# First product of each feed-forward layer by Strassen's scheme, with its operands kept in DRAM scratch

## Chip, cores and metric

The kernel runs on one core of one Trainium2 chip. The metric is the device time of one execution in microseconds (us). Three runs of the kernel before took 867.92, 869.43 and 870.33 us; the median is 869.43 us.

## What is computed

A causal retention over 4 sequences of 576 tokens, 8 heads of 64, and behind it two feed-forward layers (512 to 2048 to 512 features) on all 2304 tokens:

```python
scores = scale * np.matmul(q, k.transpose(0, 1, 3, 2))
ret = scores * Dmat[None, :, :, :]          # gamma ** (i - j) for i >= j, else 0
x = (ret @ v) as 2304 x 512
h = x @ w_in;  g = h * sigmoid(h);                              x = g @ w_out      # layer 0
h = x @ w_in;  g = np.maximum(h, 0) + alpha * np.minimum(h, 0); x = g @ w_out      # layer 1
```

The weights arrive as 64-bit floats and everything is computed to float32.

## The kernel before

**Matmuls.** Every float32 operand of the layers is split into a high part in the type fp32r and the rest, low, in the same type (ACT makes the high part by a copy, DVE the low one by a subtraction). A product is then three matmuls, high·high, low·high and high·low, each 128x128 stationary against up to 512 moving columns, accumulated in PSUM.

**Tiles and groups.** The 2304 tokens are five tiles (`TILES`, one of 256 and four of 512). Hidden features come as 16 blocks of 128 (`f`), in groups (`GROUPS`): 2, 4, 4, 4, 2 blocks in layer 0 and four times 4 in layer 1. Each group walks over all tiles, there and back. For a tile and a block, `h_unit` (L491) makes one PSUM bank of h from 4 feature chunks (12 matmuls), activates it (ACT and DVE) and splits the result g. `y_unit` (L519, layer 0, tokens as columns) and `out_unit` (L536, layer 1, 512 features as columns) multiply g by the second weights and add the group's sum to `bufb` or `bufa` on DVE (ACT copies it in the first group). The units of g are issued behind the h units of the next tile, so PE has a tile's work in hand while ACT and DVE activate.

**Weights.** `weight` (L328) loads a block of 512 KB as raw words (queue SP), makes floats of it with two ACT, three DVE and one POOL instruction (`low` by `top`), and splits it with one ACT and two DVE instructions. 64 blocks are decoded in all. `split_x` and `split_block` split the activations.

**Attention.** 18 blocks of 128 tokens run ahead of and between the units of the first group. Each loads two packs of 512 KB, is prepared on DVE, multiplied in 64x64 matmuls and split by `split_block` (L482).

**Order.** Everything is recorded by `Program` (L52) in the order of the code. PE keeps that order. For ACT, DVE, POOL and SP a planner (`order`, L144) sets each engine's order from costs and due times: of the instructions that can begin first it takes the one that is due first. It treats DVE instructions that read SBUF alone and POOL's as not running at once (`held`). `close_att` (L304) issues what is recorded so far and gives the attention's memory to the layers. Since the planner's wrapper issues all instructions, all have line 228 in the profile, and tiles tell them apart.

## Time and profile before

| | |
|---|---|
| runs | 867.92, 869.43, 870.33 us |
| profiled execution, first to last instruction (span) | 866.1 us |
| PE busy | 841.1 us (97%) |
| DVE busy | 618.9 us (71%) |
| ACT busy | 428.6 us (49%) |
| POOL busy | 94.4 us (11%) |
| DMA | 58.34 MB, mean 67 GB/s |

The profiled execution's own device time is not listed beside its span; the median of the runs is 3.3 us over the span. Busy shares are averages over the whole span; the first 110 us are attention mixed with the first group, the rest is the layers alone.

### The profile page before, as it was taken

The numbers are of one execution on the slowest core, as the hardware profiler recorded it, in microseconds if no ns is written. First come the engines' busy times: TensorE is split into PE (matmuls) and PEld (weight loads), VectorE is DVE, ScalarE is ACT, GpSimd is POOL, SyncE is SP. The second block draws the span as 40 slices with busy tenths as digits, with TensorE's granted clock in tenths as the row PEclk, the third lists the DMA queues.
The fourth block names the chain that finished last, engine by engine and source line by source line (L and its number), as shares of the span: only waits on it lengthen the run. The fifth ranks groups of instructions, "written<-read, shape, count | busy, mean of one in ns | idle before, by whom it ended". The sixth has DMA issues, their size and how long they took to land.

```text
span 866.1 us, 14498 instructions
## 1 busy us (share of the span) xinstructions
PE 841.1 (97%) x5932; PEld 707.6 (82%) x5932; DVE 618.9 (71%) x1015; ACT 428.6 (49%) x819; POOL 94.4 (11%) x68
## 2 busy tenths in 40 slices
PE   5799999999999999999999999999999999999998
PEld 4677788888988888888988888888888788888887
DVE  6988989748894798646899844884459964964443
ACT  3545575424653455324645755774344754543331
POOL 0101112101120022101001100220002210100000
PEclk9899999999999999999999999999999999999999
DMA  9856312201210032100111110220002210001111
GB/s 346 289 188 194 124 59 88 74 0 38 85 49 25 25 98 78 44 1 28 51 44 50 31 43 1 97 74 25 1 1 74 73 49 1 25 1 49 50 50 73
DMA packets 17490, 58.34 MB, mean 67 GB/s; under 512 B 2064, under 2 KB 2320, under 8 KB 17424
## 3 DMA queue, kind: packets, MB, share of 16 engines
q1 hardware_dynamic: 17424, 57.43, 19.3%
q8 instruction: 46, 0.75, 0.3%
q14 instruction: 20, 0.16, 0.1%
HBM read 52.70 MB, written 4.72 MB: 66 GB/s over the span
## 4 chain that ended last, share of the span: by engine, by line
PE 92%; DVE 4%; DMA 3%; ACT 1%; issue 1%; SPq 0%; DVEq 0%
PE bank L228 88%; DMA pack<-in_qkv 3%; PE xo L228 2%; PE sd L228 1%; DVE a L228 1%; DVE att L228 1%; DVE pack L228 1%; DVE w L228 0%; ACT bufa L228 0%; DVE g L228 0%; ACT x L228 0%; DVE act L228 0%; DVE top L228 0%; ACT act L228 0%; DVE x L228 0%
## 5 line engine op out<-in xcount | busy, mean ns | idle before, releaser
L228 PE MATMUL bank<-x,w 128*128 128x512 f32 (+1 forms) x1320 | 280.6, 369 | 1.1 <-ACT x L228 1.1
L228 PEld LDWEIGHTS bank<-x,w 128*128 128x128 f32 x1320 | 230.7, 189 | 43.1 <-ACT x L228 1.3
L228 POOL TENSOR_TENSOR low<-low,top 128x512 f32<-128x512 f32 x64 | 94.2, 1477 | 665.8 <-DVE top L228 625.6
L228 ACT ACTIVATE act<-bank 128x512 f32<-128x512 f32 (+1 forms) x160 | 88.3, 552 | 96.4 <-PE bank L228 92.8
L228 PE MATMUL bank<-x,w0b 128*128 128x512 f32 (+1 forms) x600 | 127.3, 368 | 0.0
L228 PEld LDWEIGHTS bank<-x,w0b 128*128 128x128 f32 x600 | 105.1, 189 | 19.0
L228 DVE SCALAR_TENSOR_TENSOR act<-down,nalpha_sb,act 128x512 f32<-128x512 f32 (+1 forms) x80 | 57.8, 723 | 74.1 <-ACT act L228 73.2
L228 ACT ACTIVATE down<-bank 128x512 f32<-128x512 f32 (+1 forms) x80 | 44.4, 555 | 127.7 <-PE bank L228 126.6
L228 DVE TENSOR_TENSOR bufb<-bank,bufb 128x512 f32<-128x512 f32 (+1 forms) x80 | 50.7, 635 | 43.5 <-PE bank L228 43.0
L228 PE MATMUL bank<-g,w 128*128 128x512 f32 (+1 forms) x336 | 77.9, 371 | 3.0 <-DVE g L228 1.4
L228 DVE TENSOR_TENSOR bufa<-bank,bufa 128x512 f32<-128x512 f32 (+1 forms) x55 | 37.4, 679 | 58.5 <-PE bank L228 58.3
L228 DVE TENSOR_TENSOR act<-bank,act 128x512 f32<-128x512 f32 (+1 forms) x80 | 50.7, 633 | 28.7 <-ACT act L228 28.2
L228 PEld LDWEIGHTS bank<-g,w 128*128 128x128 f32 x336 | 58.3, 195 | 14.4 <-DVE g L228 3.2
L228 ACT ACTIVATE top<-raw 128x512 f32<-128x512 f32 x64 | 42.6, 671 | 39.9 <-POOL low L228 30.6
L228 DVE TENSOR_TENSOR g<-act,g 128x512 fp32r<-128x512 f32 (+1 forms) x84 | 57.1, 684 | 6.7 <-ACT g L228 6.3
L228 PE MATMUL bank<-gb,w1b 128*128 128x512 f32 (+1 forms) x288 | 61.4, 354 | 0.0
L228 ACT ACTIVATE low<-raw 128x512 f32<-128x512 uint32 x64 | 42.7, 672 | 37.4 <-DVE w L228 22.5
L228 ACT CAST g<-act 128x512 fp32r<-128x512 f32 (+1 forms) x84 | 48.6, 581 | 18.4 <-DVE act L228 18.1
L228 PE MATMUL bank<-w,g 128*128 128x512 f32 x240 | 55.7, 390 | 0.4 <-DVE w L228 0.4
L228 PE MATMUL bank<-w1b,gb 128*128 128x512 f32 (+1 forms) x252 | 55.6, 379 | 0.0
L228 PEld LDWEIGHTS bank<-gb,w1b 128*128 128x128 f32 x288 | 48.6, 189 | 7.6
L228 DVE TENSOR_TENSOR x<-bufa,x 128x512 fp32r<-128x512 f32 (+1 forms) x82 | 53.1, 676 | 1.3 <-ACT x L228 1.3
(55 smaller groups left out, 1065.7 us busy)
## 6 DMA issues: line engine op xcount, KB each, us to landing
raw<-in_w SPq DMA_DIRECT2D x64, 512.0 KB, 3.5
pack<-in_qkv SPq DMA_DIRECT2D x26, 512.0 KB, 4.9
bufb<-in_qkv SPq DMA_DIRECT2D x10, 512.0 KB, 5.7
out<-bufa SPq DMA_DIRECT2D x17, 256.0 KB, 2.0
att<-in_small SPq DMA_DIRECT2D x1, 256.0 KB, 2.5
out<-bufa SPq DMA_DIRECT2D x2, 128.0 KB, 1.7
alpha_sb<-in_alpha SPq DMA_DIRECT2D x1, 8.0 KB, 5.6
```

Source lines behind the costliest of these rows:

```text
L228: getattr(getattr(self.nc, name), method)(*args, **kwargs)
```

## The change

The first product of each layer, but for the first two hidden blocks of layer 0, is made in units of 256 hidden features (`q`, a pair of blocks) and 768 tokens (`p`, three of them, two halves of 384). Weights and activations are cut into 2 x 2 blocks; seven block products (`product`, 6 matmuls of 384 columns each) give what eight gave. Four of the seven weight operands and four of the seven activation operands are sums or differences, formed on DVE ahead of the split. The sums of products are made partly by accumulating in PSUM, partly by three ACT copies and two DVE additions in each unit (`unit`).

- The seven activation operands (`xops`, one set) are made when a layer first meets a token group and stored in DRAM (`od`); later groups load them back. Layer 0's activations themselves go through DRAM (`xd`), one store in each attention block, one load for each token group.
- The first two hidden blocks of layer 0 run as before, on six tiles of 384 tokens. `y_unit` and `out_unit` become pieces that a queue hands out: `gaps` says how many pieces `fill` issues behind each product. Pieces of layer 0 have 384 columns, those of layer 1 still 512.
- POOL adds the low word to each decoded weight (one more POOL instruction a block); DVE then needs one subtraction for the split where it needed two instructions.
- Two short matmuls stand ahead of the first unit and touch its two PSUM banks.

```diff
-GROUPS = [(0, range(0, 2)), (0, range(2, 6)), (0, range(6, 10)), (0, range(10, 14)), (0, range(14, 16)),
-          (1, range(0, 4)), (1, range(4, 8)), (1, range(8, 12)), (1, range(12, 16))]
-TILES = [256, 512, 512, 512, 512]
-RAWS = 2
+GROUPS = [(0, [0]), (0, [1, 2]), (0, [3, 4]), (0, [5, 6]), (0, [7]),
+          (1, [0, 1]), (1, [2, 3]), (1, [4, 5]), (1, [6, 7])]
+HALF = 384
+NT6 = NT // HALF
+NPR = NT6 // 2
+BPP = 2 * HALF // P
...
+A22, A11, A12, S3, S1, S2, S4 = range(7)
+B11, T1, B21, T2, B22, T3, T4 = range(7)
...
+        nc.gpsimd.tensor_tensor(out=dst, in0=dst, in1=low, op=ALU.add)
...
+    def weights(layer, q, plain=False):
...
+        w = rings["wt"].next()
+        decode(layer, 0, 2 * q, w[:, 512:1024])
+        decode(layer, 0, 2 * q + 1, w[:, 0:512])
...
+        both = rings["w0"].next().rearrange("p (s n) -> p s n", s=2)
+        a21, a22, a11, a12 = (w[:, i * 256:(i + 1) * 256] for i in range(4))
+        split(both[:, 0, 0:768], both[:, 1, 0:768], w[:, 256:1024])
+        nc.vector.tensor_tensor(out=a22, in0=a21, in1=a22, op=ALU.add)
+        nc.vector.tensor_tensor(out=a21, in0=a11, in1=a21, op=ALU.subtract)
+        nc.vector.tensor_tensor(out=a11, in0=a22, in1=a11, op=ALU.subtract)
+        nc.vector.tensor_tensor(out=a12, in0=a12, in1=a11, op=ALU.subtract)
+        split(both[:, 0, 768:1792], both[:, 1, 768:1792], w)
+        w_pair[layer, q] = both
...
+        nc.sync.dma_start(out=home[:, :, n % BPP * P:(n % BPP + 1) * P], in_=block(n))
...
+    def operands(src):
+        b11, b12, b21, b22 = (src[:, 2 * k:2 * k + 2, j * HALF:(j + 1) * HALF] for k in range(2) for j in range(2))
+        def put(i, b):
+            hi, lo = (xops[i][:, s * 2 * HALF:(s + 1) * 2 * HALF].rearrange("p (k t) -> p k t", k=2) for s in range(2))
+            split(hi, lo, b)
+        def less(out, a, b):
+            nc.vector.tensor_tensor(out=out, in0=a, in1=b, op=ALU.subtract)
+        put(B11, b11)
+        less(b11, b12, b11)
+        put(T1, b11)
+        put(B21, b21)
+        put(B22, b22)
+        less(b12, b22, b12)
+        less(b22, b22, b11)
+        put(T2, b22)
+        put(T3, b12)
+        less(b21, b21, b22)
+        put(T4, b21)
...
+    def operands_for(layer, p, first):
+        if first:
+            if layer == 0:
+                nc.sync.dma_start(out=xs, in_=xd[p])
+                operands(xs.rearrange("p (c t) -> p c t", c=NC))
+            else:
+                operands(feat(p))
+            for i in (B11, T1, B21, T2, B22, T3, T4):
+                nc.sync.dma_start(out=od[layer][p][i], in_=f32(xops[i]))
+        elif loaded[-1] != (layer, p):
+            for i in (B11, T1, B21, T2, B22, T3, T4):
+                nc.sync.dma_start(out=f32(xops[i]), in_=od[layer][p][i])
...
+    def product(o, both, a, b, start=False):
+        w = both[:, :, a * 2 * P:(a + 1) * 2 * P]
+        x = xops[b].rearrange("p (s k t) -> p s k t", s=2, k=2)
+        for k in range(2):
+            wh, wl = (w[:, s, k * P:(k + 1) * P] for s in range(2))
+            xh, xl = x[:, 0, k], x[:, 1, k]
+            nc.tensor.matmul(o, wh, xh, start=start and k == 0, stop=False, skip_group_check=True)
+            nc.tensor.matmul(o, wl, xh, start=False, stop=False, skip_group_check=True)
+            nc.tensor.matmul(o, wh, xl, start=False, stop=k == 1, skip_group_check=True)
+    def unit(layer, q, key, fill, gaps):
+        weights(layer, q)
+        both = w_pair[layer, q]
+        f1, f2 = 2 * q, 2 * q + 1
+        a, b, d = home("a"), home("b"), home("d")
+        product(a, both, A11, B11, start=True)
+        nc.scalar.copy(b, a)
+        fill(gaps[0])
+        product(d, both, S1, T1, start=True)
+        s5 = rings["act"].next()
+        nc.scalar.copy(s5, d)
+        fill(gaps[1])
+        product(a, both, A12, B21)
+        activate(layer, f1, (*key, 0), a)
+        fill(gaps[2])
+        product(b, both, S2, T2)
+        s2 = rings["act"].next()
+        nc.scalar.copy(s2, b)
+        fill(gaps[3])
+        product(d, both, S4, B22)
+        nc.vector.tensor_tensor(out=d, in0=d, in1=s2, op=ALU.add)
+        activate(layer, f1, (*key, 1), d)
+        fill(gaps[4])
+        product(b, both, S3, T3)
+        nc.vector.tensor_tensor(out=s5, in0=b, in1=s5, op=ALU.add)
+        activate(layer, f2, (*key, 1), s5)
+        fill(gaps[5])
+        product(b, both, A22, T4)
+        activate(layer, f2, (*key, 0), b)
...
+                weight(0, f)
+            weights(0, 1)
...
+    for n, (gi, layer, qs, p) in enumerate(steps):
+        first = GROUPS[gi - 1][0] != layer or gi == 1
+        operands_for(layer, p, first)
...
+        now = with_done(woven(early[:3], 3) + flat(early[3:]), early_key, fs)
+        then = with_done(flat(late), late_key, fs)
+        if len(qs) == 2:
+            unit(layer, qs[0], (gi, p), fill, (0, 1, 1, 0, 1, 2) if layer == 0 else (0, 1, 1, 0, 1, 1))
+            queue += now[:3]
+            unit(layer, qs[1], (gi, p), fill, (1, 1, 1, 0, 1, 2) if layer == 0 else (1, 1, 0, 0, 1, 2))
+            queue += now[3:]
+            fill(len(queue))
+            queue += then```

How the change moves instructions, at three places. Names: `bank`, `sd` and `xo` are PSUM, `xop_1878` to `xop_1884` are the operands B11, T1, B21, T2, B22, T3, T4, `g` the activated h, `w` second weights (and, with `xop`, first ones), `shared` the memory of the first group's x and first weights, which later holds two of the three sets of first weights.

**PE, where the first group ends.** Before, the pieces of the last tile are followed by the h matmuls of group 1:

```order
L228 MATMUL bank_110<-g_99,w_2_87 128x512
L228 MATMUL bank_110<-g_99,w_3_88 128x512
L228 MATMUL bank_110<-g_100,w_2_87 128x512
L228 MATMUL bank_107<-x_93,w0b_1734 128x512
L228 MATMUL bank_107<-x_93,w0b_1735 128x512
L228 MATMUL bank_107<-x_94,w0b_1734 128x512
```

Now:

```order
L221 MATMUL bank_152<-g_140,w_2_127 128x384
L221 MATMUL bank_151<-shared 128x384 x12
L221 MATMUL bank_152<-shared 128x384 x12
L221 MATMUL sd<-shared 128x384 x2
L221 MATMUL bank_149<-xop_1878,w_0_124 128x384 x6
L221 MATMUL xo<-xop_1879,w_0_124 128x384 x6
L221 MATMUL bank_150<-g_141,w_0_125 128x384
```

The h matmuls of the last plain tile (24 on `shared`) stand directly ahead of the first block product. Their g is used only behind the second product.

In the second unit of the same step, with the queue of pieces empty, the last products stand without a piece between them:

```order
L221 MATMUL sd<-xop_1881,shared 128x384 x6
L221 MATMUL xo<-xop_1882,shared 128x384 x6
L221 MATMUL sd<-xop_1883,shared 128x384 x6
L221 MATMUL sd<-xop_1884,shared 128x384 x6
L221 MATMUL bank_151<-gb_1891,w_8_133 128x384
L221 MATMUL bank_151<-gb_1891,w_9_134 128x384
```

Three of the four write the same bank of `sd`, which ACT and DVE read in between.

**SP, the same stretch.** Before, behind the last packs only weights are loaded:

```order
L228 DMA bufb<-in_qkv 128x1024 x2
L228 DMA pack_116<-in_qkv 128x1024 x2
L228 DMA raw_68<-in_w 128x512
L228 DMA alpha_sb<-in_alpha 128x16
L228 DMA raw_69<-in_w 128x512
```

Now:

```order
L221 DMA pack_160<-in_qkv 128x1024 x2
L221 DMA xd_72<-xs 512x1x128 x5
L221 DMA raw_115<-in_w 128x512
L221 DMA raw_116<-in_w 128x512
L221 DMA alpha_sb<-in_alpha 128x16
L221 DMA xs<-xd_70 128x3072
L221 DMA raw_115<-in_w 128x512
L221 DMA raw_116<-in_w 128x512
L221 DMA od_0_0_73<-xop_1878 128x1536
```

The load of the first token group stands behind the stores of the last attention blocks and two weight blocks; the stores of the operands follow it on the same queue.

**DVE, the first operands.** Before, h's second tile needs four splits (`x_96<-bufa`) for 48 matmuls:

```order
L228 TENSOR_TENSOR w0b_1737<-a_76,low_72 128x512
L228 TENSOR_TENSOR x_96<-bufa,x_95 128x512
L228 TENSOR_TENSOR act_106<-bank_110,act_106 128x512
L228 TENSOR_TENSOR x_96<-bufa,x_95 128x512 x3
L228 TENSOR_TENSOR g_102<-act_105,g_101 128x512
```

Now:

```order
L221 TENSOR_TENSOR xop_1878<-xs,xop_1878 128x768
L221 TENSOR_TENSOR xs<-xs 128x2x384
L221 TENSOR_TENSOR xop_1882<-xs,xop_1882 128x768
L221 TENSOR_TENSOR xs<-xs 128x2x384
L221 TENSOR_TENSOR xop_1879<-xs,xop_1879 128x768
L221 TENSOR_TENSOR xop_1880<-xs,xop_1880 128x768
L221 TENSOR_TENSOR xs<-xs 128x2x384
```

The second product's operand (T1, `xop_1879`) is the fifth of these instructions, the third's (`xop_1880`) the sixth.

## Rows read from the trace of the kernel before

**Rows 1.** The page: busy time by engine, and the chain's shares by engine.
```profile
PE 841.1 (97%) x5932; PEld 707.6 (82%) x5932; DVE 618.9 (71%) x1015; ACT 428.6 (49%) x819; POOL 94.4 (11%) x68
PE 92%; DVE 4%; DMA 3%; ACT 1%; issue 1%; SPq 0%; DVEq 0%
```
**Rows 2.** Busy time by stretch: PE, PEld, DVE, ACT, POOL, granted clock, DMA.
```profile
27.50:55.00 27.50, 21.73 (x536) 18.22 (x536) 24.44 (x46) 14.71 (x33) 2.86 (x2) 0.88 0.64 222
140.00:650.00 510.00, 510.00 (x2443) 430.65 (x2442) 363.23 (x595) 255.64 (x479) 57.23 (x40) 1.00 0.13 43
650.00:700.00 50.00, 49.58 (x253) 42.16 (x252) 47.37 (x79) 31.09 (x64) 12.36 (x7) 1.00 0.21 73
```
**Rows 3.** The chain in order of time: start, us, what.
```profile
53.53 4.92 DMA pack<-in_qkv
...
110.14 559.81 PE bank L228 x2688
...
679.52 183.53 PE bank L228 x842
```
**Rows 4.** Timeline of PE, 200 to 245 us: start, us, what, count.
```profile
204.24 1.52 PE L228 MATMUL bank<-g,w1b 128*128 128x512 f32 x6
205.60 1.52 PE L228 MATMUL bank<-gb,w 128*128 128x512 f32 x6
...
222.39 0.88 PE L228 MATMUL bank<-g,w 128*128 128x256 f32 x6
223.11 0.88 PE L228 MATMUL bank<-gb,w1b 128*128 128x256 f32 x6
```
**Rows 5.** Groups of instructions, shapes apart: busy us, mean ns; idle before.
```profile
L228 PE MATMUL bank<-x,w 128*128 128x512 f32 x1056 | 246.7, 390 | 1.1 <-ACT x L228 1.1
L228 PEld LDWEIGHTS bank<-x,w 128*128 128x128 f32 x1320 | 230.7, 189 | 43.1 <-ACT x L228 1.3 <-DVE x L228 0.4
...
L228 PE MATMUL bank<-x,w0b 128*128 128x512 f32 x480 | 112.1, 389 | 0.0
```
**Rows 6.** Timelines of POOL and DVE in two places: start, us, what.
```profile
312.56 1.66 POOL L228 TENSOR_TENSOR low<-low,top 128x512 f32<-128x512 f32 x1 [0.42 <-DVE top L228]
...
312.99 1.78 DVE L228 TENSOR_TENSOR a<-a,w1b 128x512 f32<-128x512 f32 x1
...
332.48 0.69 DVE L228 TENSOR_TENSOR gb<-act,gb 128x512 fp32r<-128x512 f32 x1
333.08 0.69 DVE L228 TENSOR_TENSOR act<-bank,act 128x512 f32<-128x512 f32 x1
```
**Rows 7.** Groups of instructions of ACT, DVE and POOL, shapes apart.
```profile
L228 POOL TENSOR_TENSOR low<-low,top 128x512 f32<-128x512 f32 x64 | 94.2, 1477 | 665.8 <-DVE top L228 625.6 <-ACT bufa L228 27.3 <-ACT g L228 8.1
L228 DVE TENSOR_TENSOR act<-bank,act 128x512 f32<-128x512 f32 x64 | 44.0, 687 | 25.9 <-ACT act L228 25.5
L228 DVE TENSOR_TENSOR a<-a,w1b 128x512 f32<-128x512 f32 x16 | 20.4, 1292 | 0.0
L228 ACT CAST x<-bufb 128x512 fp32r<-128x512 f32 x56 | 32.4, 625 | 0.0
L228 DVE TENSOR_TENSOR act<-bank,act 128x256 f32<-128x256 f32 x16 | 6.7, 417 | 2.8 <-ACT act L228 2.8
L228 ACT CAST x<-bufb 128x256 fp32r<-128x256 f32 x12 | 4.5, 405 | 0.0
```
**Rows 8.** DMA: GB/s in 40 slices of 0:110 us; issues, us to landing.
```profile
GB/s 120 275 340 408 386 414 425 402 419 273 225 331 305 313 215 212 45 301 76 203 183 258 174 292 280 149 40 174 180 231 209 305 310 279 28 189 13 0 6 0
raw<-in_w SPq DMA_DIRECT2D x64, 512.0 KB, 3.5
out<-bufa SPq DMA_DIRECT2D x17, 256.0 KB, 2.0
```

More of the change, by code (lines that the diff above doesn't have):

```diff
@@ new lines, in h_unit @@
+    def h_unit(t, f):
+        hi, lo = x_hi[t], x_lo[t]
+        weights(0, f // 2, plain=True)
+        both = w_pair[0, f // 2]
+        o = psum()[:, 0:HALF]
+        for c in range(NC):
+            at = 512 * (1 - f % 2) + c * P
+            wh, wl = both[:, 0, at:at + P], both[:, 1, at:at + P]
+            nc.tensor.matmul(o, wh, hi[:, c], start=c == 0, stop=False)
+            nc.tensor.matmul(o, wl, hi[:, c], start=False, stop=False)
+            nc.tensor.matmul(o, wh, lo[:, c], start=False, stop=c == NC - 1)
+        activate(0, f, (0, t), o)
@@ L585, in retention_ffn_kernel @@
     att_tables()
-    hs, ys = zip(*(unit_pair(s) for s in range(len(TILES))))
     blocks = iter(range(NBLK))
@@ new lines, in retention_ffn_kernel, with fill @@
+    for i in range(2):
+        nc.tensor.matmul(homes["b"][i], first_w0[:, 0, 0:P], x_hi[NT6 - 1][:, 0], start=True, stop=True,
+                         skip_group_check=True)
+    steps = []
+    for gi, (layer, qs) in list(enumerate(GROUPS))[1:]:
+        order = range(NPR) if gi == 1 else [e[3] for e in steps[-NPR:]][::1 if GROUPS[gi - 1][0] != layer else -1]
+        steps += [(gi, layer, qs, p) for p in order]
+    queue = []
+    def fill(n):
+        while n and queue:
+            n -= 1
+            queue.pop(0)()
@@ new lines, in with_done, with woven, flat @@
+    def with_done(pieces, key, fs):
+        return pieces[:-1] + [lambda: (pieces[-1](), done(key, fs))]
+    queue += with_done(y, (0, NT6 - 1), [0, 1])
+    def woven(units, n):
+        out = []
+        for i in range(0, len(units), n):
+            for parts in zip(*units[i:i + n]):
+                out += parts
+        return out
+    def flat(units):
+        return [e for u in units for e in u]
+    for n, (gi, layer, qs, p) in enumerate(steps):
+        first = GROUPS[gi - 1][0] != layer or gi == 1
+        operands_for(layer, p, first)
+        fs = [f for q in qs for f in (2 * q, 2 * q + 1)]
+        halves = []
+        for th in range(2):
+            key = (gi, p, th)
+            if layer == 0:
+                e = [y_pieces(key, fs, p, th, m, len(qs)) for m in range(NC)]
+            else:
+                e = [out_pieces(key, fs, p, th * 3 + b, n == len(steps) - 1 and th == 0 and b == 2) for b in range(3)]
+            halves.append((e, key))
+        (late, late_key), (early, early_key) = halves
+        now = with_done(woven(early[:3], 3) + flat(early[3:]), early_key, fs)
[6 more added lines that the diff above has]
+            fill(len(queue))
+            queue += then
+        else:
+            unit(layer, qs[0], (gi, p), fill, (1, 1, 1, 0, 1, 2))
+            fill(len(queue))
+            queue += now
+            if [e[0] == gi for e in steps[n + 1:n + 3]] != [True, False]:
+                fill(len(queue))
+            queue += then
@@ L620, in retention_ffn_kernel @@
+    fill(len(queue))
     nc.issue()
```

295 lines of the change are left out of this document (149 added, 146 removed).

## The prediction, made before the change was run

> **What bounds the kernel now.** I read the page first: PE is busy 97% of the span, and the chain that ended last is PE for 92% [rows 1]. A busy PE need not be a full one, so the next question is whether it ever waits. In the chain in order of time PE runs for 559.8 us and for 183.5 us without a break; the attention ahead of that still has waits for DMA [rows 3]. From 140 to 650 us PE is busy 510 of 510 us at granted clock 1.00, which is the level of 2.4 GHz; DVE is busy for 363 of these (71%) and DMA for 0.13. The one dense stretch in which PE loses something, 650 to 700 us, is that in which DVE comes to 47.4 of 50 us [rows 2]. So in the layers time is PE's columns and nothing else, and the nearest other limit is DVE.
>
> What a matmul costs is read from the timeline, between starts: 1.36 us for six of 512 columns, 226.7 ns each; 0.72 us for six of 256, 120.0 ns each [rows 4]. Two widths give a line: 106.7 ns for 256 columns (2.4 a ns) and 13.3 ns for each matmul. At 384 columns that is **173.3 ns**. (The mean of 390 ns in the groups [rows 5] is a duration that overlaps its neighbours', not a price.)
>
> **What PE saves.** Before, the loops give 3156 matmuls of 512 columns (1536 of them h's, [rows 5]) and 600 of 256, the last output counted as halves: 3156 x 226.7 + 600 x 120.0 = 787.5 us. Now the order has 3186 of 384 (45 units x 42 = 1890, 144 of the plain first group, 1152 pieces of layer 0), 852 of 512 and 24 of 256: 3186 x 173.3 + 852 x 226.7 + 24 x 120.0 = 748.1 us. The columns fall by 103,680 (43.2 us at 2.4 a ns), and 306 more matmuls take 4 us of it back: **-39.3 us**. The two short matmuls ahead of the first unit count for nothing.
>
> **What lies beside PE.** *DVE.* Durations of 687 ns at 512 columns and 417 at 256 [rows 7] give 0.55 us at 384 and 0.96 at 768; two starts are 0.60 us apart where one lasts 0.69 [rows 6], so a queue of them moves 0.09 faster. Added: 90 additions in units (50 us); operands, 66 instructions of 768 (63 us) where some 130 splits of x by layers went; one DVE instruction for two in 64 decodes. Priced by pitch, all rows of DVE in the order come to 540 us before and 564 now, +24. POOL has 64 instructions more. A POOL instruction holds up a DVE one that meets it: 1.78 us for one that began while POOL was at work [rows 6], 1292 ns on average against 687 for the group that meets it most [rows 7], so up to 0.6 x 64 = 39 us. DVE goes from 619 us to at most 682, some 80% of the new span: not the bound on average, but it must be early where PE waits for it. *ACT* gains three PSUM copies a unit, 135 x 0.5 = 67 us, on 429 busy: covered by its idle half.
>
> *Reloads.* 84 loads of 786 KB. Each operand has one tile, so its load starts when the second unit's product has read it, and must land before the next step's first unit: 102 matmuls lie between (36 products' and 66 pieces'), 17.7 us in layer 0, 17.1 in layer 1. A 512 KB load lands in 3.5 us, and slices of DMA reach 425 GB/s [rows 8]; all seven take 12.9 us at that rate, each in turn. Cover of 17 us against a landing of 3.5 to 8: nothing. Without it, each load would cost its 5 us. The 42 stores run beside PE too, in steps of 31 us.
>
> **What comes back onto the path.** Four places, each with both ends.
>
> 1. *Attention*: 18 stores of 256 KB (`xd`) on SP between the packs. Nothing, if the packs wait for their buffers anyway; 0.62 us of transfer at 425 GB/s and some 0.33 of issue each, 18 x 0.95 = 17 us, if all lie on the path. The chain there is mostly compute, with waits such as 4.9 us for a pack [rows 3]; I take **+4**.
> 2. *The first unit.* From the last block's copy: store 2.0 us [rows 8], load of 1.57 MB (3.7 us of transfer and the 2.3 that a 512 KB load takes beyond its 1.2), two weight blocks ahead on SP (2.5), ACT split 0.83 (from 625 and 405 ns, [rows 7]): 11.3 us. PE has 42 matmuls meanwhile, 7.3 us. So 2 to 4 us, 3 taken. Then T1's low part is DVE's fifth instruction (4.4 us) and wanted 2.2 us after B11's high part: 2. In the second unit no piece stands between the last products: DVE's addition (0.55) and the activation of f2 (2.6 us against 1.7 of cover) cost 2. Sum **+7**; 3 if SP's weights come early, 16 if DVE comes to it with other work and the clock falls with the wait, as in the stretch at 0.88 [rows 2], worth 3 us.
> 3. *Layer 1's first group.* DVE's rows from one operand set to the next come to 29.3 us, 31.7 with two decodes' POOL meetings, for 30.9 us of PE. About 1 us in each of three steps, **+3**; 0 to 12.
> 4. *Every other unit.* Before the last product, DVE must have read that bank: 0.55 us behind whatever it is doing (up to 0.87), with 2.08 us of pieces as cover in layer 0 and 1.36 or 2.72 in layer 1. Only a meeting with POOL breaks it; POOL is at work a fifth of the time. 0.13 us x 45 units = **+6**; 0 to 44 (below).
>
> Sum against the profiled execution: 866.1 - 39.3 + 4 + 7 + 3 + 6 = 846.8 us of span; with the 3.3 us by which the median stands over the span, **850.1 us**.
>
> On place 4 the Trainium skill, "SBUF — State Buffer", section "SBUF: two separate sides", goes further than I do: VectorE with two SBUF inputs and GpSimd share a port pair under an exclusive lock, and the loser waits for the whole instruction. The trace agrees on the single meeting (1.78 us, rows 6). By that rule alone the 64 added instructions at 1.48 us would shut DVE out for 95 us instead of 39, and the rival that goes slower would be the likelier one; the rows' averages are what I go by.
>
> **The rivals.**
> - *All of it hidden.* DVE has 29% idle in the dense stretch, pieces cover each read, and only the first unit waits: 866.1 - 39.3 + 3 + 3.3 = 833 us. For it: not one wait of PE in 510 us [rows 2]. Against it: before, ACT and DVE had a tile's work as cover, now 1 to 2 us. **0.15**
> - *DVE locked at the gates: slower.* In each unit the addition that frees the bank for the last product meets a POOL instruction: 1.78 + 0.55 against 1.36 of cover, 0.98 us in each of 45 units, 44 us: 866.1 - 39.3 + 4 + 7 + 3 + 44 + 3.3 = 888 us. It decides against the change from (39.3 - 14) / 45 = 0.56 us a unit. For it: POOL's doubled work, and 47 of 50 us of DVE where PE does wait [rows 2]. Against it: the planner keeps such instructions apart as far as its costs are right, and waits need a coincidence. **0.13**
> - *DMA in the way.* Stores delay the packs by the full 17 us and the first unit by 16: 866.1 - 39.3 + 17 + 16 + 3 + 6 + 3.3 = 872 us, no change to measure; half as bad, 859. For it: slices of 400 GB/s in the first 25 us [rows 8]. Against: from 27 us on DMA is busy for two thirds at most. **0.11**
> - *The narrow matmul is no cheaper.* A weight load takes 189 ns [rows 5]; if it set the pace under 384 columns, 3186 x 15.7 ns = 50 us come back, 900 us. Against it: at 256 columns the pace is 120 ns with the same loads [rows 4]. **0.03**
>
> **How the numbers follow.** The forecast, 850.1 us, has 0.58, with 840 to 860 from the small terms. What a measurement of this kernel can tell from no change is 0.3%, 2.6 us. Faster: 0.58 + 0.15 + half of DMA's case = 0.79. Same: the worse half, 0.05. Slower: 0.13 + 0.03 = 0.16. The range leaves out slower (0.16) and a few hundredths at the low end, and reaches from just under the first rival to the worse half of DMA: 831 to 872 us.
>
> **What would show it.** Starts of six 384-column matmuls 1.04 us apart; the sum of PE's matmuls at 748 us. One hole of 3 to 8 us in PE behind the attention, released by `xop0` from DMA `xs`; short ones behind `sd` released by DVE. No PE wait released by DMA `xop`. DVE at about 80%. I am wrong if PE's idle time in the layers exceeds some 40 us, if 384 columns take more than 180 ns, or if the attention ends later than 115 us plus a few.

## The result, and the profile after

The changed kernel takes 879.43 us (median of 4 runs, 877.18 to 881.21); the kernel before took 869.21 us beside it. The ratio is 1.0106, 95% interval 1.0078 to 1.0134: slower by 1%, outside the predicted range. The profiled execution took 877.18 us, the fastest of the four, with a span of 875.5 us, 9.4 us more than before. The forecast is set against the traces by one measure, used in all that follows. For each 128x128 matmul of n columns, the time from its start to the next matmul's start, less the n/2.4 + 13.3 ns at which they follow when nothing waits, is called its **loss**; waits and matmuls at the lower clock both show up in it. Summed over the 4064 of them, the loss is 60.1 us after and 11.1 before.

The page, busy time by engine and the chain's shares, to be read beside [rows 1]:

```profile
PE 819.9 (94%) x6240; PEld 760.4 (87%) x6240; DVE 666.1 (76%) x1114; ACT 478.8 (55%) x947; POOL 177.3 (20%) x132
PE 75%; DVE 15%; DMA 5%; ACT 2%; issue 2%; POOL 0%; SPq 0%; DVEq 0%; ACTq 0%; POOLq 0%
```

PE has less work, but the chain that ended last is PE for 75% and no longer for 92%. The columns were saved as forecast. PE's timeline has the narrow matmuls at 1.04 us for six, 173 ns each, beside [rows 4]; further down, three of 512 columns in layer 1:

```profile
224.08 1.20 PE L221 MATMUL sd<-xop,shared 128*128 128x384 f32 x6
225.12 1.20 PE L221 MATMUL xo<-xop,shared 128*128 128x384 f32 x6
...
704.33 0.85 PE L221 MATMUL bank<-w,gb 128*128 128x512 f32 x3
705.02 0.84 PE L221 MATMUL bank<-w,shared 128*128 128x512 f32 x3
```

The trace has 3188 matmuls of 384 columns, 852 of 512 and 24 of 256, at their pitches 748 us. So all that the sum had wrong is loss: +49.0 us against -39.3 gives 9.7, and the span grew by 9.4. It lies here:

| stretch (after) | loss, us | of that in the forecast |
|---|---|---|
| attention, to 122.0 us (before: to 110.2, loss 9.8) | 20.2 | +4 |
| to the end of the first unit pair, 122 to some 174 | 17.3 | +7 |
| layer 1's first group | 6.4 | +3 |
| all other units (before: 1.3) | 16.2 | +6 |

The stretches by busy time, columns as in [rows 2], first before, then after:

```profile
36.00:110.00 74.00, 66.30 (x1724) 54.02 (x1724) 63.69 (x114) 37.27 (x76) 5.89 (x5) 0.95 0.52 172
110.00:125.00 15.00, 15.00 (x78) 12.36 (x67) 12.56 (x20) 12.35 (x23) 2.95 (x2) 1.00 0.22 72
125.00:150.00 25.00, 25.00 (x112) 20.72 (x111) 23.10 (x37) 16.10 (x30) 4.38 (x3) 1.00 0.27 85
150.00:200.00 50.00, 50.00 (x223) 41.41 (x222) 29.23 (x49) 19.37 (x36) 4.24 (x3) 1.00 0.10 32
```
```profile
36.00:110.00 74.00, 61.28 (x1483) 54.40 (x1473) 59.18 (x107) 38.65 (x81) 16.82 (x12) 0.93 0.69 230
110.00:125.00 15.00, 14.50 (x353) 13.20 (x353) 14.68 (x24) 9.01 (x19) 5.98 (x4) 1.00 0.23 62
125.00:150.00 25.00, 19.79 (x94) 17.63 (x93) 22.52 (x30) 17.17 (x33) 5.77 (x4) 0.86 0.95 363
150.00:200.00 50.00, 43.89 (x244) 41.52 (x243) 42.85 (x71) 30.50 (x56) 5.43 (x4) 1.00 0.74 279
200.00:650.00 450.00, 439.48 (x2381) 417.87 (x2381) 362.51 (x612) 259.22 (x505) 114.22 (x84) 1.00 0.51 187
650.00:850.00 200.00, 200.00 (x999) 179.80 (x998) 127.53 (x216) 105.28 (x220) 23.14 (x17) 1.00 0.39 141
```

Before, DVE was just as full from 125 to 150 us and PE did not wait: what DVE did there was not yet wanted. From 150 to 200 us it now has 42.9 us of work in 50, where it had 29.2. From 36 to 110 us, in the attention, it is less busy than before (59.2 us for 63.7): what PE waits for there is not the amount of DVE's work alone.

Three places of the chain and the timelines show what PE waits for. In the attention the chain in order of time (start, us, what) runs through the first group's weights, by way of POOL's new addition:

```profile
39.45 1.28 POOL low L221
40.73 1.69 POOL wk L221
...
42.44 0.63 ACT w L221
...
43.09 1.55 DVE w L221
...
49.29 0.70 DVE w L221
...
50.03 2.29 PE bank L221 x6
...
122.50 2.71 DMA xd<-xs
...
125.27 7.54 DMA xs<-xd
```

POOL's multiplication and addition take 3 us of that chain, and what follows is a queue on DVE. The last two rows are the trip of the activations through DRAM behind the attention's last copy: 10.3 us, where the prediction had 8.0 for store and load and 2.5 for two weight blocks ahead. PE's hole there was 3.73 us, ended by ACT's `xop`:

```profile
133.76 0.62 PE L221 MATMUL bank<-xop,w 128*128 128x384 f32 x2 [3.73 <-ACT xop L221]
```

Then the places at which DVE meets POOL (start, us, instruction; POOL first):

```profile
141.24 1.29 POOL L221 TENSOR_TENSOR low<-low,top 128x512 f32<-128x512 f32 x1 [9.02 <-ACT xop L221]
142.61 1.89 POOL L221 TENSOR_TENSOR wt<-wt,low 128x512 f32<-128x512 f32 x1
...
141.28 4.03 DVE L221 TENSOR_TENSOR xop<-xs,xop 128x768 fp32r<-128x768 f32 x2 [0.18 <-ACT xop L221]
...
264.27 1.46 POOL L221 TENSOR_TENSOR wt<-wt,low 128x512 f32<-128x512 f32 x1
...
264.53 1.75 DVE L221 TENSOR_TENSOR w<-wk,w 128x512 fp32r<-128x512 f32 x1
...
264.04 0.34 PE L221 MATMUL bank<-g,w 128*128 128x384 f32 x1
266.34 5.98 PE L221 MATMUL bank<-g,w 128*128 128x384 f32 x20 [1.96 <-DVE w L221]
```

Two DVE instructions that take 0.95 us each elsewhere take 4.03 us together, and the second ends 0.8 us behind POOL's second. At 264 us a subtraction of 0.68 us takes 1.75, PE waits 1.96 us for it, and the next 20 matmuls take 5.98 us where 3.5 would do at the higher clock (the granted clock is 0.70 from 266.5 to 269 us and 0.68 to 272).

### The profile page after: what moved, and what is told of

Same layout as the page of the kernel before. It is cut to its first block, busy times and chain, and to the rows that moved or that the text cites. A ratio compares the mean times of both kernels' runs of the same rounds, so it can differ in the third digit from the quotient of the medians.

```text
span 875.5 us, 15664 instructions
## 1 busy us (share of the span) xinstructions
PE 819.9 (94%) x6240; PEld 760.4 (87%) x6240; DVE 666.1 (76%) x1114; ACT 478.8 (55%) x947; POOL 177.3 (20%) x132
## 4 chain that ended last, share of the span: by engine, by line
PE 75%; DVE 15%; DMA 5%; ACT 2%; issue 2%; POOL 0%; SPq 0%; DVEq 0%; ACTq 0%; POOLq 0%
PE bank L221 51%; PE sd L221 14%; PE xo L221 11%; DMA xs<-xd 2%; DMA raw<-in_w 2%; DVE wt L221 1%; DVE xop L221 1%; DVE shared L221 1%; DVE actb L221 1%; DVE wk L221 1%; DVE att L221 1%; DVE act L221 1%; DVE pack L221 1%; DVE g L221 1%; DVE w L221 1%
## 5 line engine op out<-in xcount | busy, mean ns | idle before, releaser
L221 POOL TENSOR_TENSOR low<-low,top 128x512 f32<-128x512 f32 x64 | 86.2, 1357 | 554.4 <-DVE top L221 519.8
L221 PE MATMUL bank<-g,w 128*128 128x384 f32 x588 | 133.6, 350 | 13.2 <-DVE w L221 6.1
L221 PEld LDWEIGHTS bank<-g,w 128*128 128x128 f32 x588 | 108.3, 196 | 18.3 <-DVE w L221 7.4
L221 DVE TENSOR_TENSOR ybuf<-bank,ybuf 128x384 f32<-128x384 f32 (+2 forms) x151 | 90.1, 599 | 37.2 <-PE bank L221 35.6
L221 PE MATMUL sd<-xop,shared 128*128 128x384 f32 x540 | 108.9, 336 | 4.0 <-DVE actb L221 1.7
L221 PE MATMUL bank<-w,g 128*128 128x512 f32 (+1 forms) x402 | 110.0, 391 | 1.1 <-DVE g L221 0.8
L221 PE MATMUL bank<-gb,w 128*128 128x384 f32 x456 | 102.7, 337 | 5.4 <-DVE gb L221 3.0
L221 PE MATMUL bank<-w,gb 128*128 128x512 f32 (+1 forms) x384 | 105.6, 390 | 0.2 <-DVE gb L221 0.2
L221 PEld LDWEIGHTS sd<-xop,shared 128*128 128x128 f32 x540 | 95.4, 188 | 9.1 <-DVE actb L221 2.5
L221 PEld LDWEIGHTS bank<-gb,w 128*128 128x128 f32 x456 | 80.7, 188 | 8.6 <-DVE gb L221 4.8
L221 PEld LDWEIGHTS bank<-w,g 128*128 128x128 f32 x402 | 73.7, 188 | 14.6 <-DVE g L221 2.4
L221 PEld LDWEIGHTS bank<-w,gb 128*128 128x128 f32 x384 | 70.8, 188 | 14.8 <-DVE gb L221 1.2
L221 PE MATMUL bank<-xop,shared 128*128 128x384 f32 x360 | 72.6, 335 | 0.4 <-DVE shared L221 0.4
L221 PE MATMUL xo<-xop,shared 128*128 128x384 f32 x360 | 72.1, 334 | 0.0
L221 PEld LDWEIGHTS bank<-xop,shared 128*128 128x128 f32 x360 | 63.8, 188 | 2.9 <-DVE shared L221 0.7
L221 PEld LDWEIGHTS xo<-xop,shared 128*128 128x128 f32 x360 | 63.5, 188 | 0.8
L221 PE MATMUL sd<-xop,w 128*128 128x384 f32 x270 | 54.4, 335 | 0.9 <-DVE actb L221 0.9
L221 ACT ACTIVATE top<-raw 128x512 f32<-128x512 f32 x64 | 42.9, 673 | 20.3 <-DMA raw<-in_w 14.1
L221 ACT COPY sd<-bank 128x384 f32<-128x384 f32 x45 | 21.0, 466 | 59.1 <-PE bank L221 56.1
L221 PEld LDWEIGHTS sd<-xop,w 128*128 128x128 f32 x270 | 47.6, 188 | 2.9 <-DVE actb L221 1.1
L221 POOL TENSOR_TENSOR wt<-wt,low 128x512 f32<-128x512 f32 x32 | 46.6, 1468 | 1.1
L221 POOL TENSOR_TENSOR wk<-wk,low 128x512 f32<-128x512 f32 x32 | 45.2, 1433 | 0.3
## 6 DMA issues: line engine op xcount, KB each, us to landing
raw<-in_w SPq DMA_DIRECT2D x64, 512.0 KB, 4.4
pack<-in_qkv SPq DMA_DIRECT2D x36, 512.0 KB, 6.2
xd<-xs SPq DMA_DIRECT2D x18, 256.0 KB, 5.5
out<-ybuf SPq DMA_DIRECT2D x17, 256.0 KB, 2.3
att<-in_small SPq DMA_DIRECT2D x1, 256.0 KB, 2.8
```

The lines of the kernel that those rows point to most:

```text
L221: getattr(getattr(self.nc, name), method)(*args, **kwargs)
```

## The experiments

Each ratio is to the kernel before, run on the same chip beside it. "End" is the end of the attention, "first" the start of the first block product, then the loss in the attention, in the first step (units of the first token group) and from the attention's end to the last matmul, all of the profiled execution. Those columns are of one execution each: in e2a it lies 4.5 us under that kernel's median, in e2 2.9 us over it, so differences of 2 or 3 us between rows say little there.

| kernel | us | ratio, 95% interval | end | first | loss: attention | first step | all layers |
|---|---|---|---|---|---|---|---|
| the change | 879.4 | 1.0106 [1.0078, 1.0134] | 122.0 | 133.8 | 20.2 | 13.2 | 39.9 |
| e1 | 869.1 | 1.0011 [0.9991, 1.0030] | 121.5 | 133.9 | 10.5 | 13.4 | 30.1 |
| e2a | 877.5 | 1.0087 [1.0055, 1.0120] | 119.8 | 131.4 | 16.1 | 13.5 | 37.9 |
| e2 | 873.0 | 1.0046 [1.0030, 1.0062] | 121.8 | 129.7 | 20.6 | 19.3 | 38.6 |
| e3 | 878.0 | 1.0097 [1.0075, 1.0119] | 122.1 | 134.2 | 19.3 | 11.3 | 34.0 |
| f1 | 865.6 | 0.9951 [0.9923, 0.9978] | 118.3 | 126.3 | 9.6 | 17.7 | 30.0 |
| f3 | 854.3 | 0.9822 [0.9789, 0.9854] | 118.2 | 130.1 | 12.8 | 8.0 | 21.3 |
| f4 | 865.3 | 0.9941 [0.9922, 0.9961] | 118.0 | 126.0 | 11.5 | 13.1 | 32.6 |
| f6 | 894.0 | 1.0276 [1.0252, 1.0300] | 118.8 | 143.7 | 16.8 | 25.4 | 60.7 |
| g1 | 861.4 | 0.9911 [0.9892, 0.9929] | 120.0 | 130.0 | 10.3 | 15.2 | 26.3 |
| g2 | 858.6 | 0.9866 [0.9839, 0.9893] | 115.1 | 122.7 | 11.2 | 12.9 | 28.5 |
| g3 | 858.7 | 0.9875 [0.9854, 0.9896] | 115.8 | 123.5 | 12.1 | 13.6 | 28.4 |
| g4 | 869.1 | 0.9986 [0.9970, 1.0001] | 128.5 | 137.8 | 14.4 | 15.0 | 25.5 |
| h1 | 848.2 | 0.9747 [0.9723, 0.9771] | 115.0 | 122.7 | 12.5 | 7.8 | 17.8 |
| h2 | 878.3 | 1.0092 [1.0062, 1.0123] | 118.5 | 130.7 | 15.3 | 19.1 | 43.5 |
| h3 | 854.7 | 0.9816 [0.9786, 0.9846] | 115.5 | 123.2 | 10.3 | 12.5 | 25.0 |

**e1: POOL's new addition goes to DVE.**
```diff
-        nc.gpsimd.tensor_tensor(out=dst, in0=dst, in1=low, op=ALU.add)
+        nc.vector.tensor_tensor(out=dst, in0=dst, in1=low, op=ALU.add)
```


> The low word is added to each decoded weight on DVE again, not on POOL (POOL back to 64 instructions, DVE 64 more of about 0.6 us). If POOL's second instruction is what costs (it lengthens the weight chain at 39 to 43 us, where PE waited 4.25 us for DVE w, and holds up DVE for 1.4 to 1.8 us in the layers): PE's waits on DVE w and DVE g shrink, attention ends 3 to 5 us earlier, the layers lose 5 to 10 us less, 866 to 872 us in all. If DVE's amount of work is what costs, 64 x 0.6 = 38 us more of it: PE waits grow and the time goes to 882 to 895 us. If neither matters (the waits are those of the operands and their DMA): 877 to 882 us.

Measured: 869.1 us, no difference from the kernel before that can be told. DVE has 64 additions of 0.68 us more (43.5 us) and is busy for 672.5 us instead of 666.1: so POOL's additions had held it up for 37 us. (Counted one by one, what DVE's instructions take beyond their group's usual time where a POOL instruction runs beside them is some 59 us in the change and 26 in e1, 33 less.) The span falls by 10.4 us, and the layers' loss by 9.8. The attention's loss halves as well, but it ends only 0.5 us sooner: the waits go from the 128x128 matmuls to the attention's small ones, which loss does not count (the time from each of these to the next matmul sums to 56.3 us in the change and to 65.7 in e1), and stand behind another instruction of DVE:

```profile
113.80 1.13 PE L221 MATMUL sd<-pack 64*64 64x64 f32 x32 [3.01 <-DVE pack L221]
```

**e2a and e2: the DRAM trip.** In e2a `xd` has the layout of `xs`, so that rows are 2 KB and not 512 bytes. In e2, on top, group 1 begins with the token group that the attention made last and that is still in `xs`; it is neither stored nor loaded (the two `if` lines and the order are e2's).
```diff
-        nc.sync.dma_start(out=home[:, :, n % BPP * P:(n % BPP + 1) * P], in_=block(n))
+        at = n % BPP * DM
+        if n < NBLK - BPP:
+            nc.sync.dma_start(out=xd[n // BPP][:, at:at + DM], in_=xs[:, at:at + DM])
...
-        order = range(NPR) if gi == 1 else [...]
+        order = [NPR - 1, *range(NPR - 1)] if gi == 1 else [...]
...
-                nc.sync.dma_start(out=xs, in_=xd[p])
+                if p < NPR - 1:
+                    nc.sync.dma_start(out=xs, in_=xd[p])
```


> Layer 0's activations go to and from DRAM in the layout in which they lie on the chip: 18 stores in pieces of 2 KB instead of 512 B; DVE and ACT read the operand blocks by a longer pattern. If small pieces hold up the packs in the attention (a store took 5.5 us to land, a pack 6.2 where it was 4.9): stores land in 2 to 3 us, attention ends 3 to 6 us earlier, 872 to 876 us. If the attention's loss comes from the weights' chain (POOL, DVE): attention ends at 122 us as now and the time stays within 2 us, 877 to 881.

> As the block layout, and the first token group of group 1 is the one whose activations still lie in xs: no load before the first unit, and the 6 stores of that group are left out (12 stay). If the trip through DRAM is what makes the first step dear (2.7 us for the last store, 7.5 for the load, then operands one after the other, and PE's clock down behind the wait): the wait of 3.9 us ahead of the first product goes, the step loses 8 to 10 us less, 867 to 872 us. If DVE's and ACT's operand work is what costs there, it only begins earlier: the hole moves to T1 and T2, 2 to 4 us gained, 875 to 878.

Measured: the layout alone does nothing that can be told (the load takes 8.3 us for 8.7). Without the trip, the wait ahead of the first product is gone and the product starts 4 us sooner, but in the profiled execution the same step then loses 6 us more, 5.12 of them PE waiting for the second pair's weights, while POOL needs 5.05 us for two instructions that take it 1.3 each alone. The median is 6.4 us under the change's, between the ranges of the two theories; the profiled execution, one of the slowest, does not show where the rest was gained:

```profile
148.74 0.69 PE L221 MATMUL bank<-xop,shared 128*128 128x384 f32 x1 [5.12 <-ACT shared L221]
...
137.83 5.05 POOL L221 TENSOR_TENSOR low<-low,top 128x512 f32<-128x512 f32 x2 [21.11 <-DVE top L221]
```

**e3: 26 short matmuls in place of 2 ahead of the first unit,** in the hole, to hold the clock.

```diff
-    for i in range(2):
+    for i in (0, 1) * 13:
```


> 26 short matmuls instead of 2 ahead of the first unit, 24 x 0.173 = 4.2 us of PE work into the wait of 3.9 us; nothing else. If the granted clock that falls with the waits is a good part of the first step's loss (about 6 of its 17 us are matmuls that take longer than 173 ns): the products behind it run at full speed and 3 to 5 us come back, 873 to 877 us. If the losses are the waits themselves: no gain, 0 to 1 us more, 878 to 882.

```profile
125.00:150.00 25.00, 21.41 (x117) 19.77 (x117) 22.47 (x29) 17.23 (x33) 6.42 (x4) 1.00 0.94 359
```

Measured: the granted clock of this stretch is 1.00 and not 0.86, and the time falls by 1.5 us, within the two intervals. That step's loss falls by 1.9 us (13.2 to 11.3), so the clock was at most a small part of it.

**f1: e1 and e2 together; f4: f1 with the planner's costs of POOL and DVE set by the trace; f3: the changed kernel without the low word of the weights, which its output then lacks; f6: the changed kernel without decoding ahead in the attention** (each weight is then decoded where it is first used). Of f3, f4 and f6:
```diff
-        nc.scalar.activation(low, lower.bitcast(U32), AF.Copy, scale=2.0 ** -52)
...
-        nc.vector.tensor_scalar(out=top.bitcast(I32), in0=a, scalar1=-2 ** 23, ...)
-        nc.gpsimd.tensor_tensor(out=low, in0=low, in1=top, op=ALU.mult)
-        nc.gpsimd.tensor_tensor(out=dst, in0=dst, in1=low, op=ALU.add)
...
-            return 140 + (0.56 if len(reads) < 2 and not psum else 1.075) * n
+            return 70 + (0.52 if len(reads) < 2 and not psum else 1.035) * n
...
-            return 100 + 2.1 * n
+            return 100 + 2.5 * n
...
-            for f in range(2, 6):
-                weight(0, f)
-            weights(0, 1)
```


> Two edits together, each tried alone before: the second POOL operation of a weight put on DVE, and the resident pair first in group 1 (contiguous DRAM layout with it). Theory A (two separate costs: the POOL addition lengthens each weight's chain and holds DVE; the start of group 1 waits for a DRAM trip): the gains add, 869.1 and 873.0 against 879.4, so 862 to 865, with no PE wait of over 2 us between the end of the attention and the first product, and the excess of the first step under 10 us (19.3 with the order alone, 13.4 with the addition alone). Theory B (one cost: at the start of group 1 DVE has more work than PE has matmuls, whichever operand is late): the hole moves again, first step still over 13 us, time 867 to 870.

> This kernel leaves out the low word of every weight (ACT's conversion of it, DVE's masking, POOL's multiplication and addition), so that POOL does nothing in the layers and a weight's chain is four operations shorter; the output lacks that part of the weights. Theory A (POOL and its lock on DVE are most of the lost 50 us): excess of the matmul time from 60 to under 30 us, the attention's end from 122 to under 116, and 845 to 855 us. Theory B (DRAM trip, clock and the order of the attention carry most): the attention still ends after 118, first step still loses 10 us or more, and the time is 860 or more, little under the 869 of the kernel with the addition on DVE.

> As the kernel with both edits (addition on DVE, resident pair first), and the planner's costs set by this trace: POOL 100 + 2.5 n ns, DVE 70 + 1.035 n or 70 + 0.52 n. If the planner's order (decided with POOL and DVE priced wrongly) puts pieces of the attention or of the weights too late, the same work is 2 to 6 us faster than the kernel without this edit; if only the amount of work before the first product counts, the two are within 1.5 us of each other.

> Only edit to the changed kernel: the decoding of group 1's weights (second weights of features 2 to 5, first weights of pair 1) isn't recorded inside the attention, but after it where it is first used. Theory A (this decoding, now with more DVE and POOL work each, is what makes the attention end at 122 instead of 110): the attention ends at 112 to 116, but the first products then wait for weights, 5 to 15 us. Theory B (the attention is late by the weights of its own first group and by DVE work per block): it ends within 2 us of 122. The total in either case 876 to 888.

Measured: f1 is faster than the kernel before. No wait of over 2 us is left ahead of its first product, as theory A of that run had it, but its first step still loses 17.7 us, as theory B had it, and the time (865.6) lies between the two ranges. The planner's costs are worth nothing that can be told. Without any low word (f3) the time is 854.3, in theory A's range, but the whole loss is 34.1 us and not under 30, and the attention ends at 118.2 and not under 116: its end is not POOL's alone. Without decoding ahead (f6) it ends at 118.8, which neither theory had, and the time, 894.0, is beyond the range of both (876 to 888), since PE pays for it behind:

```profile
143.67 0.69 PE L221 MATMUL bank<-xop,w 128*128 128x384 f32 x1 [16.98 <-ACT w L221]
```

**g1: f1 with POOL's old multiplication on DVE too. g2: g1 with two weights fewer decoded in the attention. g3: g2 with a second tile `wt`. g4: g1 with the very first pair split feature by feature.**
```diff
-        nc.gpsimd.tensor_tensor(out=low, in0=low, in1=top, op=ALU.mult)
+        nc.vector.tensor_tensor(out=low, in0=low, in1=top, op=ALU.mult)
...
-            for f in range(2, 6):
+            for f in range(2, 4):
...
-    rings["wt"].grow(big, "wt", 1024, 1)
+    rings["wt"].grow(big, "wt", 1024, 2)
...
-        rings["act"].grow(pool, "actb", HALF, 4)
+        rings["act"].grow(pool, "actb", HALF, 3)
...
-            split(first_w0[:, 0], first_w0[:, 1], w)
+            for at in (512, 0):
+                split(first_w0[:, 0, at:at + 512], first_w0[:, 1, at:at + 512], w[:, at:at + 512])
```


> Base: the kernel with the addition on DVE and the resident pair first (865.6 us). Only edit: POOL's multiplication of the weights' low word is also put on DVE, so that POOL has no operation on SBUF in the layers; DVE gets 64 operations of about 0.68 us (43 us) and loses the stretches in which it is held by POOL (64 operations of 1.4 us). Theory A (what POOL costs is the hold on DVE and the longer chain, not its own time): DVE's operations of 1.2 us and more disappear, the second operand-free stretch behind the first product improves, 859 to 864. Rival (DVE is the bound from 36 to 150 us by amount, and 43 us more of it cost more than the holds): 867 to 872.

> As the kernel with everything on DVE, and the second weights of features 4 and 5 are not decoded inside the attention but where group 1's second half first uses them; the attention then decodes four weights ahead, as many as in the kernel before, in place of six. If that count is what makes the attention end at 118 to 122 in place of 110, it ends 2 to 4 us earlier than in the kernel without this edit; the total is 1 to 4 us shorter if the two decodings find a place before their use, and no shorter, with a larger excess in the first two steps, if DVE is full from the attention to the second step.

> As the kernel with the two deferred weights, and a second tile for the decoding of a pair (paid for with one of the activations' tiles), so that the next pair can be decoded while the last is still being split. If the single tile holds the next pair back, the holes by ACT and DVE 'shared' (the second pair's weights, 5 us in the first step) go and the time falls by 2 to 5 us; if DVE's amount of work holds it back, no change within 1.5 us.

> As the kernel with everything on DVE, and the very first pair of weights (group 0, not combined) is split feature by feature in place of both together. If the start of the attention's matmuls (31.3 us, 25.2 before) waits for the second feature's decoding, the first of them starts 3 to 6 us earlier; it shortens the attention by as much only if TensorE is what ends it, otherwise the attention ends within 1 us of the kernel without this edit.

Measured: g1 gains 4 us (0.9911 against 0.9951; the intervals just meet), and DVE, with 64 instructions of 0.68 us more, is busy for only 15.5 us more. In g2 the attention ends at 115.1, 5 us sooner, and the time is 2.8 us lower (the intervals of g1 and g2 touch at their ends). A second `wt` tile changes nothing (858.7 for 858.6), so the tile does not hold the second pair back; that DVE's work does was left to h1. (In g3 seven tiles are left for activations, so in layer 1 the third activation of each unit overwrites `s5` with its first half before its second half has read it, and that part of the result differs.) g4 missed both its cases: the first matmul on `shared` does not move (31.3 us), and the attention takes 8 us longer. At 44 us PE waits for a sum of the attention (`att`), behind eight instructions on weights that DVE did first; how the rest of the 8 us arises was not followed:

```profile
43.87 0.71 PE L221 MATMUL xo<-pack,att 64*64 64x64 f32 x16 [2.66 <-DVE att L221]
```

**h1: g2 with the operands' low parts written by ACT as copies, so that DVE loses work in a stretch of its own (their correction is left out of the result). h2: the changed kernel with two weights fewer decoded ahead, alone. h3: g2 with a third tile for raw weights** (of h1 and h3; h2's edit is the second one of g2).
```diff
-            split(hi, lo, b)
+            nc.scalar.copy(hi, b)
+            nc.scalar.copy(lo, b)
...
-    rings["raw"].grow(big, "raw", 512, 2, I64)
+    rings["raw"].grow(big, "raw", 512, 3, I64)
...
-        rings["act"].grow(pool, "actb", HALF, 4)
+        rings["act"].grow(pool, "actb", HALF, 3)
...
-            nc.scalar.activation(dn, o, AF.Relu, scale=-1.0)
             nc.scalar.activation(g, o, AF.Relu)
+            nc.scalar.activation(dn, o, AF.Relu, scale=-1.0)
```


> Base: the kernel with everything on DVE, the resident pair first and two weights deferred (858.6 us, 12.9 us of excess in its first step, DVE busy 24.4 of the 25 us from 125 to 150). Edit: the seven low words of a pair's operands are written as copies by ACT in place of differences by DVE, so that their correction is left out of the result; DVE loses 7 operations of 0.95 us per prepared pair, ACT gets 7 of 0.8 us. Theory A (the amount of DVE's work is what bounds the first step): its excess falls from 12.9 to 5 to 8 us and the time to 850 to 855. Theory B (a late operand, a queue or the clock behind the waits): the excess stays within 2 us of 12.9 and the time within 2 us of 858.6.

> Only edit to the changed kernel: the second weights of features 4 and 5 are decoded where they are first used, so that the attention decodes four weights ahead as before, not six. Theory A (the two more decodings, with POOL's two operations each, are part of the attention's late end): it ends at 118 to 120 in place of 122, and the time is 874 to 878. Theory B (the attention is late by the first pair of weights and by the planner's order): it ends within 1 us of 122, and the time is 879 to 884, since the two decodings then stand in the first step.

> As the kernel with everything on DVE, resident pair first and two weights deferred, and a third tile for the raw words (with one of the activations' tiles less, and the two halves of layer 1's activation computed in the other order so that this is safe). If the 3.3 us hole at 252 us comes from a raw load that could only be issued when the tile came free and then lay beside the reloads (8.2 us from issue to landing), that hole and the slow matmuls behind it go, and the time is 852 to 856; if the load is late by the reloads alone, no change within 1.5 us.

Measured, the stretch from 125 to 150 us in g2 and then in h1:

```profile
125.00:150.00 25.00, 20.17 (x89) 17.68 (x90) 24.44 (x43) 15.00 (x30) 0.00 (x0) 0.86 0.93 335
```
```profile
125.00:150.00 25.00, 21.11 (x109) 17.98 (x107) 21.66 (x40) 22.61 (x43) 0.00 (x0) 1.00 0.96 340
```

The first step's loss falls from 12.9 to 7.8 us, as theory A had it; the layers' as a whole by 10.7, and the time by 10 us, more than expected, since the fourth step (5.8 to 1.0 us) and layer 1's first gain too. The same operands come from the same places; DVE has less to do and ACT more. So 5 of that step's 13 us go with DVE's work on the operands. The handover from ACT to DVE between an operand's two parts goes as well, and the run does not tell it from the amount; the other 8 us were not taken apart. In h2 the attention ends 3.5 us sooner and the first step loses 5.9 more, and the time, 878.3, is the change's within the noise: moving the two decodings gained nothing, though DVE is busy for only 7.5 of the 15 us from 110 to 125 there. In g2 a hole at 252 us was the one place where a load was in the way: the chain has `raw` landing 8.18 us after its issue, beside the reloads. With the third tile PE's wait there goes from 3.32 to 1.56 us, that step's loss from 5.8 to 2.7, and the median falls by 3.9 us (the two intervals just overlap). The chain in g2 and PE's row behind it, then PE's row in h3:

```profile
244.03 0.41 ACT actb L221
244.43 8.18 DMA raw<-in_w
...
255.64 6.07 PE L221 MATMUL bank<-g,w 128*128 128x384 f32 x21 [3.32 <-ACT g L221]
```
```profile
253.93 4.71 PE L221 MATMUL bank<-g,w 128*128 128x384 f32 x21 [1.56 <-ACT g L221]
```

h3 is the version to keep: 854.7 us, 1.8% below the kernel before (0.9786 to 0.9846), with POOL idle. It has 15 to 16 us of the 39 that the columns give.

## Why the prediction was wrong, point by point

The 39.3 us of columns came; the four waits put at 4 + 7 + 3 + 6 = 20 us came to 49.0. The step that failed is how DVE was judged: by a mean share ("some 80% of the new span: not the bound on average") and by single waits at a few places. The sum has no term for the first group's weights waiting in chains of DVE and POOL, and one of 4 us for the first unit's work on DVE, which is busy for 37.2 of the 40 us from 110 to 150. Of the prediction's own signs of being wrong, the attention's end is the one that came: 122 us for "115 plus a few".

**What PE saves** was right: count, pitch and sum (748 us). So was *the narrow matmul is no cheaper* as an unlikely rival. In layer 1, matmuls of 512 columns follow at 230 ns for 227, some 3 us in all that were not foreseen and that no run explains.

**Reloads** were right for this kernel: 84 loads land in 5.9 us in the median, within "3.5 to 8", and no wait of PE in the layers ended with `xop` from DMA. The cover had no room for the raw loads beside them, which showed only when other waits were gone (g2).

**Place 1, the attention**, failed: +4 forecast, +10.4 us of loss measured, and an end at 122 and not 110. The step that failed is its cause. I priced the stores `xd` alone. Nothing in the chain there was an `xd`; the waits were weights and the attention's own sums on DVE. The change decodes six weights in the attention for four (two weight blocks of pair 1 and four of the second product), a count in the code that I did not take. Two fewer gave 5 us at the attention's end in g2 and 3.5 in h2 (in h2 the first step took them back). POOL's addition on the first group's weight chain had 10 us of the loss, but without it the end stayed where it was, the waits having gone to the attention's small matmuls (e1). What holds the end at 115 in the best version, past the 2.7 us of matmuls that the attention has more of (38.6 us at their pitches for 35.9), is open.

**Place 2, the first unit**, failed by size: +7 forecast and at most 16, 17.3 measured. The hole of the DRAM trip came out as forecast (3.7 us for 2 to 4), but the rest of the sum took DVE's work of one unit. DVE has a set of operands (11 instructions of 0.95 us), the rest of two pairs of weights and the activations to do in 25 to 30 us, so taking the trip away moved the wait to the second pair (e2), while taking away DVE work shortened the step (h1, f3). That is the case which the prediction put at 16, "if DVE comes to it with other work and the clock falls with the wait": e3 puts the clock at some 2 us of it; of the rest, the 5 us that h1 took away with DVE's work are shown, in a later version of the kernel.

**Place 3**: +3, measured 6.4, within 0 to 12.

**Place 4** failed in place and size: +6 forecast, 16.2 measured, of which 7.3 are left without POOL's addition (e1), some 3 of these the 230 ns of layer 1. The hold itself was sized well: up to 39 us forecast for POOL's 64 new instructions, 37 measured (e1). But the gates at which I let it act were not where PE paid. For DVE's addition that frees a bank ahead of the last product PE waited four times where it writes `actb` (us in total, times, longest), and once more, 1.6 us at 165.9, where it writes `act`; 2.5 of these 4.3 us are behind the first step:

```profile
PE sd L221 <- DVE actb L221: 2.7, 4, 1.5
```

And that addition itself, the first of these groups, is not held. Groups of DVE instructions in the changed kernel, shapes apart, and the last three of them again in g2, where POOL is idle:

```profile
L221 DVE TENSOR_TENSOR actb<-sd,actb 128x384 f32<-128x384 f32 x33 | 18.3, 555 | 7.4 <-PE sd L221 4.9 <-ACT actb L221 2.4
L221 DVE TENSOR_TENSOR g<-act,g 128x384 fp32r<-128x384 f32 x55 | 36.4, 665 | 2.6 <-ACT g L221 2.0
L221 DVE TENSOR_TENSOR xop<-ybuf,xop 128x768 fp32r<-128x768 f32 x21 | 22.3, 1067 | 2.2 <-ACT xop L221 2.1
L221 DVE TENSOR_SCALAR wt<-top 128x512 int32<-128x512 int32 x32 | 16.8, 539 | 4.4 <-ACT top L221 4.3
```
```profile
L221 DVE TENSOR_TENSOR g<-act,g 128x384 fp32r<-128x384 f32 x55 | 30.3, 552 | 3.5 <-ACT g L221 3.5
L221 DVE TENSOR_TENSOR xop<-ybuf,xop 128x768 fp32r<-128x768 f32 x21 | 19.8, 952 | 0.3 <-ACT xop L221 0.2
L221 DVE TENSOR_SCALAR wt<-top 128x512 int32<-128x512 int32 x32 | 12.5, 421 | 2.1 <-ACT top L221 2.1
```

The first reads PSUM and takes 555 ns, and 556 in g2; the next two read SBUF twice and go from 665 to 552 ns and from 1067 to 952 when POOL is idle. [Rows 7] had shown as much: 687 ns for `act<-bank`, 1292 for `a<-a,w1b`. The fourth has one SBUF input and is held too, 539 ns for 421. The Trainium skill, "SBUF — State Buffer", section "SBUF: two separate sides", gives the lock for two SBUF inputs against a GpSimd instruction that reads SBUF, and for a 2-port perf mode: the first three groups agree, and whether the fourth is in such a mode no run shows. The prediction's 95 us by that rule took DVE to want the ports all the time; the 64 instructions cost it 37 us and the kernel 10. What POOL cost PE came through chains: weights that were a POOL instruction longer, or held at a split (264 us), and late activations (`w`, `g`, `gb`) in front of pieces. From 174 to 400 us these waits come to 6.1 us, and in e1 to 1.0.

**The rivals.** *DVE locked at the gates* had the right sign and the right pair of engines, with its price at the wrong instructions: 44 us at the gates, where PE waited 4.3. *All of it hidden* rested on DVE's 29% of idle time in the dense stretch [rows 2]; more than half of the new loss (27.7 of 49 us) came in the first 174 us, where DVE's share before was not 71% but 86% from 36 to 110 us (63.7 of 74) and 92% from 125 to 150 (23.1 of 25).

## What to carry to other kernels

An engine's mean share over the span says nothing of a start-up stretch: lay the new work of each engine against the time of that stretch, and count there all that the change moves into it, decodings ahead of use included. Before handing work to POOL to relieve DVE, look which DVE instructions POOL's hold up, here those with two SBUF inputs and the one-input `wt<-top`, not those that read PSUM: 64 additions moved back to DVE, at 43.5 us of its time, made the kernel 10 us faster. When one wait is removed and another of the same engine's work appears behind it, as in e1's attention and in e2, count the amount of that work before going on to the next wait.

## What the runs showed of the hardware that was not expected

- A POOL instruction too is held: 3.08 and 2.01 us for two in e2 from 137.8 us, 1.27 to 1.30 us for seven of the same kind beside which no DVE instruction ran in the changed kernel.
- A DVE instruction with one SBUF input (`wt<-top`) is held by POOL as well: 539 ns in the mean, 421 with POOL idle.
- DMA at 167 MB and 191 GB/s, three times the 58 MB of before, ended no wait of PE in the layers behind the first step (the chain has one load there, a `raw` of 6.03 us at 442 us); rows of 512 bytes in DRAM against 2 KB made no difference that could be told (8.7 us to landing, and 8.3).
- 24 added matmuls brought the granted clock from 0.86 to 1.00 for 25 us and gained no time that can be told (e3), since the work behind them was late anyway.
